# Linear attention into a one-of-eight expert layer on one core: where the scatters of sorted rows stand in the unit loop, row products in pairs, denominators from two tensors

## The chip, the core and the metric

One core of one Trainium2 chip runs the whole program in one launch. The metric is the device time of an execution in microseconds; lower is better. The time before is the median of three runs. Engines are named as in the profile: PE is TensorE, DVE is VectorE, ACT is ScalarE, POOL is GpSimd, SP is SyncE.

## What is computed

Attention without a softmax over 8 batches, 8 heads, 576 positions and 64 features, then a layer in which each of the 4608 tokens goes to one of eight experts:

```python
def phi(x, c, s):                       # c, s: cosine and sine of the position
    r = np.maximum(x, 0.0)
    return np.concatenate([r * c, r * s], axis=-1)
kv = np.einsum('bhsf,bhsd->bhfd', phi(k), v)
num = np.einsum('bhsf,bhfd->bhsd', phi(q), kv)
den = np.einsum('bhsf,bhf->bhs', phi(q), phi(k).sum(2))[..., None] + 1e-06
x = (num / den), one row of 512 per token
e = argmax(x @ w_gate);  gate = softmax(x @ w_gate)[e];  eom = sigmoid(x @ w_output_gate)[e]
out = gate * eom * (relu(x @ w1[e]) @ w2[e])      # w1[e]: 512x1024, w2[e]: 1024x512
```

## The kernel before

**Stages.** The program has two stages that overlap at their seam. In the attention stage the 4608 tokens are 36 units of 128 rows, four groups of nine units, two batches to a group; `n` is the unit's place in its group, 0 to 8. In the expert stage 39 tiles of 128 sorted rows pass through `layer1` and `layer2`. The tiles 0 to 10 (`EARLY`) are made up of rows of the first two groups alone; tile 11 is the first that may hold rows of the last group, so its fetch waits until all the scatters of that group have landed.

**A unit** (the loop over `units` at the end of the function) issues, in this order: `q_mm` (PE products of q with kv at L515, their evacuation by ACT at L520 and DVE at L522 into one of two buffers `u`), `aheads(i + 1)` (the weighting of the next unit's k: `k_ahead`, a `tensor_scalar` on DVE at L343 for each of two or three chunks, or an activation on ACT at L340), the transposes of q two units ahead, then the scatters that stand in this unit, `q_out` where `n` is 1, 3, 5, 7 or 8, and at the end the PE products of k and v (`k_do`, L378) and the loads. In the last group there is no k left to weight.

**q_out** turns a pair of units into rows. DVE adds 1e-6 to the denominators (L542, a `tensor_scalar` on 128x16), takes the reciprocal (L543), and makes the gate logits (L554, L558). POOL multiplies each unit's 512 columns by the reciprocals into `xrows` (L530, `q_rows`), which I call a row product: two of them for `n` = 1, 3, 5, 7 and one for `n` = 8. `between` puts one scatter between the two.

**Routing.** When the nine units of a group are done, `route` computes each row's expert and place in small DVE steps over the next units (L570 to L616). Nine scatters of one group's rows (`scatter`, L629, an indirect DMA on POOL of 128 rows of 516 two-byte words) then run during the next group, from xrows to the sorted table `xs` in DRAM. xrows has two buffers, so the first write of a later group (L541) waits until the scatters from that buffer have landed.

**Loads.** q, k, v and the rows of a tile (`fetch`, L763) are loaded by SP's queue. The weights of an expert (`load_w`, 16 loads of 1 MB at L237 and L240) are issued by POOL, in the same instruction stream and on the same software DMA queue as the scatters and as the writes of the output rows (L874). `wload` names the unit behind which each load stands: the first behind unit 22, the second behind 23, then 25, 27, 29, 31 and 33. I write W1, W2, ... for them in this order.

**What sets the order.** Each engine runs its instructions in the order in which the Python code issues them (`manual_schedule`). Two tables say how many scatters stand in a unit: `nsc` for the second and third group, `nsc2` for the last. Before, with the scatter between the two row products added, the nine scatters of a group stand at `n` = 3, 4, 5, 6, 7, 8 with 2, 1, 2, 1, 2, 1 of them.

Of the kernel before, what the change touches and what calls it, by code (L numbers as in the profile page):

```python
# [16 lines left out]
ALU = mybir.AluOpType  # L17
# [5 lines left out]
def kernel(  # L23
# [14 lines left out]
    DVE = nc.vector  # L38
# [234 lines left out]
    if True:  # L273
# [63 lines left out]
        def k_ahead(b, c, act):  # L337

            if act:
                ACT.activation(kcs[:, :, c, :], kbuf[b % 2][:, :, c, :], AF.Relu,  # L340
                               scale=cosc[:, c:c + 1])
                return
            DVE.tensor_scalar(kcs[:, :, c, :], kbuf[b % 2][:, :, c, :], cosc[:, c:c + 1],  # L343
                              0.0, ALU.mult, ALU.max)

# [189 lines left out]

        def q_out(g, u, glog, xrows, slot, n, between=None, late=None):

            rc = wk.tile([P, 2 * H], F32, name=f"rc{g}_{slot}", tag="rc")
            m = n * H
            if slot == 0:  # L540
                GP.tensor_copy(xrows[:, :, DM:DM + 2].bitcast(I32), ids[:, g, :].unsqueeze(2))  # L541
            DVE.tensor_scalar_add(rc[:, 0:m], u[:, 0:m, 64], 1e-6)  # L542
            DVE.reciprocal(rc[:, 0:m], rc[:, 0:m])  # L543
            for x in range(n):
                if x and between:
                    between()
                if late is None:
                    q_rows(GP, u, rc, xrows, slot, x)
                else:
                    late.append((u, rc, xrows, slot, x))  # L550
# [69 lines left out]

        def scatter(g, c):

            di, meta, xrows, c0, c1 = scat[g]
            if c == c0:
                GP.tensor_copy(xrows[:, c0:c1, DM + 2:DM + 4].bitcast(F32),
                               meta[:].unsqueeze(2))
            else:
                GP.nop()
            d = GP.indirect_dma_start(  # L629
                out=xs[:, :],  # L630
                out_offset=bass.IndirectOffsetOnAxis(ap=di[:, c - c0:c - c0 + 1], axis=0),
                in_=xrows[:, c, :], in_offset=None)


            tc.declare_no_dep(d.ins, group="sc", reason="distinct rows")
            tc.declare_no_dep(d.ins, group="early", reason="distinct rows")
            tc.add_to_no_dep_group("sc", d.ins)
            if g == NG - 1:
                last_sc.append(d.ins)
# [272 lines left out]

        def aheads(i):
            for n, x in enumerate(kwork[i] if i < NU else ()):
                k_ahead(*x, 20 <= i <= 27 and n == 1)

# [55 lines left out]

        nsc = {3: 1, 4: 1, 5: 1, 6: 1, 7: 1, 8: 1}
        nsc2 = {3: 1, 4: 2, 5: 1, 6: 1, 7: 1}
        outs = []
        for i, (b, c) in enumerate(units):
# [13 lines left out]
            q_mm(i, u, c % 2)  # L990
            aheads(i + 1)
            if i + 2 < NU:
# [18 lines left out]

            def scatter_next():
                nonlocal scd
                if scd < GC:
                    scatter(g - 1, scd)
                    scd += 1

            if g > 0:
                for _ in range((nsc2 if g == 3 else nsc).get(n, 0)):
                    scatter_next()  # L1020
            if c == 4 or c % 2 == 1:
                slot = 8 if c == 4 else 4 * (b % 2) + c - 1
                out_args = (g, u, glog, xrows, slot, 1 if c == 4 else 2,
                            scatter_next if g > 0 and n in (3, 5, 7) else None)
                if i < NU - 2:
                    q_out(*out_args)
                else:
                    outs.append(out_args)
            assert n < 8 or i == NU - 1 or g == 0 or scd == GC
            if n == 8:  # L1030
# [144 lines left out]
```

## Time and profile before

| what | value |
|---|---|
| three runs | 315.11 us median, 313.14 to 316.8 |
| the profiled execution | 313.45 us |
| its span, first to last instruction | 311.6 us |
| granted TensorE clock, mean | 0.984 |
| PE busy | 280.5 us (90%) |
| ACT busy | 179.9 us (58%) |
| DVE busy | 175.7 us (56%) |
| POOL busy | 130.2 us (42%) |

The profiled execution is 1.66 us under the median of the runs, and 1.85 us of it lie outside the span. The attention stage takes about the first 149 us and the expert stage the rest. A busy engine is not always a working one: an instruction that is held on its way counts as busy for as long as it is held, so the length of one instruction against the usual length of its group is as telling as the idle time.

### The profile page before, as it was taken

The page shows a single profiled execution, that of the slowest core. Times are in us where ns is not written, and L with a number is a line of the kernel's source. Part 1 is how long each engine was busy: PE and PEld are TensorE (multiplying, and loading weights), DVE is VectorE, ACT ScalarE, POOL GpSimd, SP SyncE. Part 2 cuts the span into 40 slices and gives each one's busy share as a digit, 9 for nine tenths or more (in the row PEclk, how much of TensorE's full clock was granted, in tenths as well). Part 3 has the DMA queues.
Part 4 walks back from the last instruction along what each step waited for, and adds up shares of the span by engine and source line. Part 5 has one row for each costly group of instructions (what it writes and reads, how often), then busy time and mean ns, then how long its engine had stood idle before and what let it go on. Part 6 is the DMA issues. An engine that isn't in the chain of part 4 may idle for free. (4 is left out here: it accounts for less than half of the span.)

```text
span 311.6 us, 10152 instructions
## 1 busy us (share of the span) xinstructions
PE 280.5 (90%) x3615; PEld 179.8 (58%) x3615; DVE 175.7 (56%) x510; ACT 179.9 (58%) x355; POOL 130.2 (42%) x169
## 2 busy tenths in 40 slices
PE   6788799899998877997989899999999999999991
PEld 2667687687777656765545445555544444444450
DVE  7536767789998999897688313333312222222231
ACT  4388689897989887875532333334354444444420
POOL 7003333147854878078766734062122222231322
PEclk9799799999999999999999999999999999999997
DMA  7999677869795899999998899999997878776522
GB/s 252 361 389 360 182 196 242 287 188 327 234 352 162 258 267 271 249 207 265 245 226 251 144 247 255 241 243 243 281 272 175 180 187 167 185 180 148 152 68 82
DMA packets 50976, 71.84 MB, mean 231 GB/s; under 512 B 23374, under 2 KB 30062, under 8 KB 49904
## 3 DMA queue, kind: packets, MB, share of 16 engines
q1 hardware_dynamic: 40608, 40.17, 44.7%
q0 software_dynamic: 10320, 31.01, 41.0%
q8 instruction: 32, 0.52, 0.7%
q14 instruction: 16, 0.13, 0.1%
HBM read 67.58 MB, written 16.17 MB: 269 GB/s over the span
## 5 line engine op out<-in xcount | busy, mean ns | idle before, releaser
L863 PE MATMUL yp<-wt,hts 128*128 x312 | 73.4, 379 | 0.1
L829 PE MATMUL hp<-wt,xts 128*128 x304 | 71.8, 379 | 1.2 <-issue 1.2
L839 ACT ACTIVATE hs<-hp 128x1024 f16<-128x1024 f32 x38 | 38.9, 1024 | 43.9 <-PE hp L829 43.9
L530 POOL TENSOR_TENSOR xr<-wt,rc 128x512 f16<-128x512 f32 x33 | 37.1, 1133 | 48.4 <-DVE rc L543 48.1
L870 DVE TENSOR_SCALAR ysp<-yp,xg 128x512 f32<-128x512 f32 x24 | 18.0, 751 | 69.7 <-PE yp L863 69.7
L515 PE MATMUL qo<-kvm,wt 64*64 64x162 f32 x1024 | 44.6, 306 | 8.6 <-DVE wt L522 3.4
L863 PEld LDWEIGHTS <-hts 128*128 128x128 f16 x312 | 30.4, 98 | 36.4 <-DMA hts<-hs 0.5
L794 ACT COPY xts<-xtsp 128x512 f16<-128x512 f16 x39 | 22.8, 586 | 44.5 <-PE xtsp L778 41.9
L378 PE MATMUL kvp<-wt 64*64 64x132 f32 x1152 | 42.4, 286 | 5.8 <-DVE wt L350 3.3
L829 PEld LDWEIGHTS <-xts 128*128 128x128 f16 x312 | 29.1, 98 | 29.8 <-issue 1.2
L520 ACT ACTIVATE wt<-qo,cosq 128x324 f32<-128x324 f32 x72 | 36.1, 530 | 14.8 <-PE qo L515 14.4
L522 DVE SCALAR_TENSOR_TENSOR wt<-qo,sinq,wt 128x324 f32<-128x324 f32 x72 | 36.9, 550 | 12.9 <-ACT wt L520 11.0
L515 PEld LDWEIGHTS qo<-kvm,wt 64*64 64x64 f32 x1024 | 35.5, 134 | 13.0 <-DVE wt L522 5.8
L378 PEld LDWEIGHTS kvp<-wt 64*64 64x64 f32 x1152 | 34.2, 137 | 11.6 <-issue 4.7
L874 POOL DMA_INDIRECT out_dram<-ysp,sidx x17 | 16.8, 986 | 46.5 <-DVE sidx L798 36.8
L333 ACT ACTIVATE wt<-wt,tanc 128x256 f32<-128x256 f32 x63 | 28.4, 513 | 1.3 <-DMA wt<-in_v_dram 1.3
L870 DVE TENSOR_SCALAR ysb<-yp,xg 128x512 f32<-128x512 f32 x15 | 11.2, 750 | 27.8 <-PE yp L863 27.8
L343 DVE TENSOR_SCALAR wt<-wt,cosc 128x256 f32<-128x256 f32 x56 | 24.4, 477 | 0.0
L480 ACT ACTIVATE qr<-wt 128x512 f32<-128x512 f32 x32 | 20.7, 646 | 3.6 <-DMA wt<-in_q_dram 3.6
L874 POOL DMA_INDIRECT out_dram<-ysb,sidx x11 | 10.8, 984 | 26.1 <-DVE ysb L870 14.6
L492 PE MATMUL qtp<-ident,qr 128*128 128x128 f32 x128 | 21.3, 290 | 0.2 <-ACT wt L333 0.2
L495 ACT COPY wt<-qtp 128x512 f32<-128x512 f32 x32 | 18.9, 590 | 1.7 <-PE qtp L492 1.2
(262 smaller groups left out, 312.2 us busy)
## 6 DMA issues: line engine op xcount, KB each, us to landing
wt<-in_moe_w_dram POOLq DMA_DIRECT2D x16, 1024.0 KB, 12.9
wt<-in_k_dram SPq DMA_DIRECT2D x16, 576.0 KB, 9.1
wt<-in_v_dram SPq DMA_DIRECT2D x16, 576.0 KB, 7.5
wt<-in_q_dram SPq DMA_DIRECT2D x16, 576.0 KB, 11.1
xg<-xs SPq DMA_DIRECT2D x43, 129.0 KB, 6.7
xs<-zt SPq DMA_DIRECT2D x9, 129.0 KB, 6.2
hts<-hs SPq DMA_TRANSPOSE x19, 3.3
out_dram<-ysp,sidx POOLq DMA_INDIRECT x17, 3.0
```

Of the source, the lines that this page charges most:

```text
L333: d = ACT.activation(tvs[:, c, :, 1:65], vbuf[b % 2][:, :, c, :], AF.Copy, scale=tanc[:, c:c + 1])
L343: DVE.tensor_scalar(kcs[:, :, c, :], kbuf[b % 2][:, :, c, :], cosc[:, c:c + 1], 0.0, ALU.mult, ALU.max)
L378: mm = PE.matmul(outs(i, mp), kcs[rows, m, c, :], mov, start=first, stop=(c == NCH - 1), skip_group_check=True)
L515: PE.matmul(qo[64 * l:64 * l + 64, 2 * mp + ih, 0:162], qT[r, hf, ih, l, :], kvms[b if c < 4 else b - 1 + l][r, n0:n0 + 2, :], start=True, ...
L520: d0 = ACT.activation(t, qo[:, :, 0:81], AF.Copy, scale=cosq[:, c:c + 1])
L522: d1 = DVE.scalar_tensor_tensor(u[:, h0:h0 + 4, :], qo[:, :, 81:162], sinq[:, c:c + 1], t, ALU.mult, ALU.add)
L530: e.tensor_tensor(xrows[:, slot + x, 0:DM].bitcast(F16).rearrange("p (h d) -> p h d", d=D), u[:, 8 * x:8 * x + 8, 0:64], rc[:, 8 * x:8 * x ...
L829: mm = PE.matmul(hps[fh], xts[:, kc, :], wt[:, bass.ds(ev, 1), kc * F + fh * 512:kc * F + fh * 512 + 512], start=(kc == 0), stop=(kc == 3))
L839: ACT.activation(hv, hp.rearrange("p (q c) -> p c q", c=8), AF.Relu)
L863: mm = PE.matmul(yp, hts[:, fc, :], wt[:, bass.ds(ev, 1), 4 * F + fc * DM:4 * F + fc * DM + DM], start=(fc == 0), stop=(fc == 7))
L870: DVE.tensor_scalar(ysb, yp, xg[:, DM + 2:DM + 4].bitcast(F32), None, ALU.mult)
L874: d = GP.indirect_dma_start(out=out[:, :], out_offset=bass.IndirectOffsetOnAxis(ap=idx, axis=0), in_=ysb, in_offset=None, bounds_check=N - ...
```

## The change

It does three things. `scatter` gets a further argument, the last weighting of k that DVE does in this unit, and waits for it by a semaphore. The scatters are issued at the end of a unit's `q_out`, three at a time, at `n` = 4, 6 and 8 (in the last group 4, 6 and 7, where no weighting is left to wait for), and no longer between the two row products. And the denominators come from a `scalar_tensor_tensor`, (u + 1e-6) times a tensor of ones, in place of `tensor_scalar_add`.

```diff
@@ k_ahead
             if act:
                 ACT.activation(kcs[:, :, c, :], kbuf[b % 2][:, :, c, :], AF.Relu,
                                scale=cosc[:, c:c + 1])
-                return
-            DVE.tensor_scalar(kcs[:, :, c, :], kbuf[b % 2][:, :, c, :], cosc[:, c:c + 1],
-                              0.0, ALU.mult, ALU.max)
+                return None
+            return DVE.tensor_scalar(kcs[:, :, c, :], kbuf[b % 2][:, :, c, :],
+                                     cosc[:, c:c + 1], 0.0, ALU.mult, ALU.max).ins
@@ q_out
-            DVE.tensor_scalar_add(rc[:, 0:m], u[:, 0:m, 64], 1e-6)
+            DVE.scalar_tensor_tensor(rc[:, 0:m], u[:, 0:m, 64], 1e-6, onesf[:, 0:m],
+                                     ALU.add, ALU.mult)
             DVE.reciprocal(rc[:, 0:m], rc[:, 0:m])
             for x in range(n):
-                if x and between:
-                    between()
@@ scatter
-        def scatter(g, c):
+        def scatter(g, c, behind=None):
...
+            if behind is not None:
+                tc.add_manual_dep(d.ins, behind.name, mybir.DependencyInfo(
+                    mybir.DependencyClass.Sync, mybir.DependencyReason.DATA),
+                    reason="behind the weighting of k")
@@ the loop over units
-        nsc = {3: 1, 4: 1, 5: 1, 6: 1, 7: 1, 8: 1}
-        nsc2 = {3: 1, 4: 2, 5: 1, 6: 1, 7: 1}
+        nsc = {4: 3, 6: 3, 8: 3}
+        nsc2 = {4: 3, 6: 3, 7: 3}
...
-            aheads(i + 1)
+            weighted = aheads(i + 1)
...
-            if g > 0:
-                for _ in range((nsc2 if g == 3 else nsc).get(n, 0)):
-                    scatter_next()
...
+            if g > 0:
+                for _ in range((nsc2 if g == 3 else nsc).get(n, 0)):
+                    scatter(g - 1, scd, weighted)
+                    scd += 1
```

Two places show what this does to POOL's instructions. The first is the third group, from its pair of row products at `n` = 3 to W2. Before, POOL has there:

```order
L530 TENSOR_TENSOR xr_1627<-wt,rc_2_1910 128x512
L629 DMA xs<-xr_1000,di@1_0_1851 36992x516
L231 TENSOR_LOAD ordi
...
L237 DMA wt<-in_moe_w_dram 128x4x1024
L629 DMA xs<-xr_1000,di@1_0_1851 36992x516
L530 TENSOR_TENSOR xr_1627<-wt,rc_4_2060 128x512
L629 DMA xs<-xr_1000,di@1_0_1851 36992x516
L530 TENSOR_TENSOR xr_1627<-wt,rc_4_2060 128x512
...
L240 DMA wt<-in_moe_w_dram 128x4096
```

After the change POOL has, from the same pair on (line numbers of `scatter` are one less):

```order
L530 TENSOR_TENSOR xr_1627<-wt,rc_2_1908 128x512 x2
L624 COPY xr_1000<-meta@1_0_1854 128x9
L628 DMA xs<-xr_1000,di@1_0_1851 36992x516 x3
L231 TENSOR_LOAD ordi
...
L237 DMA wt<-in_moe_w_dram 128x4x1024
L530 TENSOR_TENSOR xr_1627<-wt,rc_4_2058 128x512 x2
...
L240 DMA wt<-in_moe_w_dram 128x4096
L628 DMA xs<-xr_1000,di@1_0_1851 36992x516 x3
```

The three scatters ahead of W1 (L237) stand together right in front of it, behind the weighting of k of that unit, where before two of them were issued earlier and apart. W1 itself keeps its place behind the third scatter, and the pair of row products follows it as a whole.

The second place is the seam, on POOL again, from the fourth group's pair at `n` = 5 over W7 (L237) to the second write of output rows (L874). Before:

```order
L530 TENSOR_TENSOR xr_2305<-wt,rc_4_2785 128x512
L629 DMA xs<-xr_1627,di@2_0_2625 36992x516
...
L237 DMA wt<-in_moe_w_dram 128x4x1024
L629 DMA xs<-xr_1627,di@2_0_2625 36992x516 x2
L625 COPY xr_2305<-meta@3_0_3005 128x4
L629 DMA xs<-xr_2305,di@3_0_3002 36992x516 x2
...
L240 DMA wt<-in_moe_w_dram 128x4096
L874 DMA out_dram<-ysb_3100,xg_2315 4608x512
L629 DMA xs<-xr_2305,di@3_0_3002 36992x516 x2
L874 DMA out_dram<-ysb_3202,xg_2326 4608x512
```

And after the change:

```order
L530 TENSOR_TENSOR xr_2305<-wt,rc_4_2781 128x512 x2
L628 DMA xs<-xr_1627,di@2_0_2625 36992x516 x3
...
L237 DMA wt<-in_moe_w_dram 128x4x1024
L628 DMA xs<-xr_1627,di@2_0_2625 36992x516 x3
L624 COPY xr_2305<-meta@3_0_3005 128x4
L628 DMA xs<-xr_2305,di@3_0_3002 36992x516 x2
...
L240 DMA wt<-in_moe_w_dram 128x4096
L877 DMA out_dram<-ysb_3100,xg_2315 4608x512
L628 DMA xs<-xr_2305,di@3_0_3002 36992x516 x2
L877 DMA out_dram<-ysb_3202,xg_2326 4608x512
```

One scatter of the third group's rows has moved from ahead of W7 to behind it, and all six scatters now follow the pair at `n` = 5, where before three of them stood ahead of its second product.

## Rows read from the trace of the kernel before

**Rows 1.** A stretch: length, busy PE PEld DVE ACT POOL, clock, DMA share, GB/s

```profile
192.00:306.00 114.00, 113.15 (x665) 56.89 (x662) 32.86 (x70) 46.11 (x57) 31.04 (x33) 1.00 0.82 196
```

**Rows 2.** Timeline of PE: start, length, instruction, count, idle time before and its releaser

```profile
108.42 1.33 PE L515 MATMUL qo<-kvm,wt 64*64 64x162 f32 x32 [0.98 <-DVE wt L522]
...
113.70 0.77 PE L442 MATMUL kvtp<-ident,wt 128*128 128x128 f32 x4 [0.69 <-DVE wt L425]
...
116.08 1.33 PE L515 MATMUL qo<-kvm,qTt 64*64 64x162 f32 x32 [0.55 <-DVE wt L522]
...
121.32 0.93 PE L515 MATMUL qo<-kvm,wt 64*64 64x162 f32 x20 [1.68 <-DVE kvm L463]
```

**Rows 3.** The same of PE in the last group

```profile
142.07 1.19 PE L515 MATMUL qo<-kvm,wt 64*64 64x162 f32 x28 [1.65 <-DVE wt L522]
```

**Rows 4.** The weighting of k by itself: duration in ns, least, median, greatest

```profile
L343 DVE TENSOR_SCALAR wt<-wt,cosc x56: 340/347/1898, 21.4 to 124.3; 128x256 f32<-128x256 f32 x56
```

**Rows 5.** Timeline of DVE, third group and start of the fourth

```profile
104.78 0.77 DVE L343 TENSOR_SCALAR wt<-wt,cosc 128x256 f32<-128x256 f32 x1
...
111.42 1.90 DVE L343 TENSOR_SCALAR wt<-wt,cosc 128x256 f32<-128x256 f32 x1
...
119.09 1.89 DVE L343 TENSOR_SCALAR wt<-wt,cosc 128x256 f32<-128x256 f32 x1
...
121.10 0.46 DVE L542 TENSOR_SCALAR rc<-wt 128x8 f32<-128x8 f32 x1
...
136.67 1.01 DVE L522 SCALAR_TENSOR_TENSOR wt<-qo,sinq,wt 128x324 f32<-128x324 f32 x2
...
137.81 1.44 DVE L573 TENSOR_TENSOR sh@3_0_2735<-glog,lmax@3_0_2733 128x32 f32<-128x32 f32 x1
...
139.84 1.70 DVE L582 TENSOR_TENSOR oh<-iota8m,ei@3_0_2740 128x32 f16<-128x32 f32 x1
```

**Rows 6.** Timeline of POOL: scatters, row products and weight loads

```profile
105.55 1.01 POOL L629 DMA_INDIRECT xs<-xr,di@1_0_1851  x1 [0.17 <-issue]
106.56 0.82 POOL L237 DMA_DIRECT2D wt<-in_moe_w_dram  x1
...
119.76 1.06 POOL L530 TENSOR_TENSOR xr<-wt,rc 128x512 f16<-128x512 f32 x1
120.75 0.81 POOL L237 DMA_DIRECT2D wt<-in_moe_w_dram  x1
...
133.60 0.20 POOL L541 COPY xr<-ids 128x9 int32<-128x9 int32 x1 [9.10 <-DMA xs<-xr,di@1_0_1851]
...
139.37 1.04 POOL L629 DMA_INDIRECT xs<-xr,di@2_0_2625  x1 [0.18 <-issue]
140.42 1.07 POOL L530 TENSOR_TENSOR xr<-wt,rc 128x512 f16<-128x512 f32 x1
...
152.72 0.96 POOL L629 DMA_INDIRECT xs<-xr,di@2_0_2625  x1 [0.30 <-issue]
...
165.07 0.99 POOL L874 DMA_INDIRECT out_dram<-ysb,xg  x1 [1.24 <-DMA xs<-xr,di@2_0_2625]
```

**Rows 7.** DMA queues from 100 to 110 us: packets, MB, share of 16 engines

```profile
q1 hardware_dynamic: 945, 2.05, 71.6%
q0 software_dynamic: 100, 0.28, 7.9%
```

**Rows 8.** The same from 110 to 134 us

```profile
q0 software_dynamic: 1601, 4.62, 89.6%
```

**Rows 9.** Waits of SP's queue: what waited for what, us in total, times, longest

```profile
SPq L763 <- DMA xs<-xr,di@3_4_3187: 12.0, 1, 12.0
```

**Rows 10.** Timeline of SP at the fetch of tiles 11 and 12

```profile
184.18 1.50 SPq L763 DMA_DIRECT2D xg<-xs  x2
```

**Rows 11.** The fetch by itself, all tiles: time to landing

```profile
DMA to landing us min/median/max: 2.1/6.7/11.2
```

**Rows 12.** Timeline of PE: the transposes of tile 11

```profile
191.87 0.39 PE L778 MATMUL xtsp<-ident,xg 128*128 128x128 f16 x4
```

More of the change, by code (lines that the diff above doesn't have):

```diff
@@ L534, in q_rows, with q_out @@
                 ALU.mult)
-        def q_out(g, u, glog, xrows, slot, n, between=None, late=None):
+        def q_out(g, u, glog, xrows, slot, n, late=None):
             rc = wk.tile([P, 2 * H], F32, name=f"rc{g}_{slot}", tag="rc")
@@ L913, in aheads @@
         def aheads(i):
+            last = None
             for n, x in enumerate(kwork[i] if i < NU else ()):
-                k_ahead(*x, 20 <= i <= 27 and n == 1)
+                last = k_ahead(*x, 20 <= i <= 27 and n == 1) or last
+            return last
         def k_do(i):
@@ L1010 @@
                 next(first_half)
[L1012 to L1016, printed above, removed]
-            if g > 0:
-                for _ in range((nsc2 if g == 3 else nsc).get(n, 0)):
-                    scatter_next()
             if c == 4 or c % 2 == 1:
                 slot = 8 if c == 4 else 4 * (b % 2) + c - 1
-                out_args = (g, u, glog, xrows, slot, 1 if c == 4 else 2,
-                            scatter_next if g > 0 and n in (3, 5, 7) else None)
+                out_args = (g, u, glog, xrows, slot, 1 if c == 4 else 2)
                 if i < NU - 2:
```

## Prediction

> **What bounds the kernel now.** I read the stretches first. From 192 us on PE is busy 113.15 of 114.00 us [rows 1]: the expert stage from tile 11 to the end is PE's and nothing in the change touches it. So the end moves by as much as tile 11 moves, which starts at 191.87 [rows 12]. Two chains meet there, and the later one decides.
>
> Chain A is PE's own work before it. PE's timeline shows where PE stood waiting for DVE in the third and fourth group: 0.98 + 0.69 + 0.55 + 1.68 + 1.65 = 5.55 us [rows 2, 3]. DVE's timeline shows why: a weighting of k takes 0.35 us [rows 4], but 0.77, 1.90 and 1.89 in front of these waits, and two steps of the routing with two inputs in SBUF take 1.44 and 1.70 [rows 5]. POOL's timeline beside it: the weighting of 119.09 ends at 120.98, just behind the row product that began at 119.76 and took 1.06, and the step of 139.84 lasts through the rest of a scatter, 139.37 to 140.41, and through the row product on its heels until 141.49 [rows 5, 6]. DVE is held while POOL runs a scatter and the row product behind it, both in one.
>
> Chain B is the software DMA queue. Tile 11 may hold rows of the last group, so SP's queue stood 12.0 us for the last scatter before it fetched it at 184.18 [rows 9, 10]. With the median 6.7 us to landing [rows 11] the rows are there at 190.9, 1.0 us before PE wants them. So B has 1.0 us of room, and whatever A gains is worth 1.0 us at most unless B moves as well. B reaches back far: the queue shows 89.6% of the engines' time from 110 to 134 us, 4.62 MB or 0.19 MB per us [rows 8], and 7.9% from 100 to 110 [rows 7]. It fills up with W1, issued at 106.56, and from there POOL waits for landings: 9.10 us for the second group's last scatter until 133.60, and 1.24 us at 165.07 [rows 6].
>
> **The change, part by part.** The work is the same: 27 scatters in the unit loop, 20 denominators, the same row products and loads. What it moves:
>
> Chain A. Without a scatter between, a pair of row products takes 2 x 1.06 = 2.1 us from the reciprocal on, against 1.06 + 0.17 + 1.01 + 1.06 = 3.3.
> - PE's wait at 108.42: the weighting at 104.78 was held 0.77 - 0.35 = 0.42 us by a row product that now ends earlier. Some of it goes back to the scatters that now stand there; I take 0.3 us back.
> - 113.70 and 116.08: the weighting at 111.42 was held 1.55. Now W1 is out only at 109.6 (below), the pair follows until 111.7, and the weighting, due at about 111.1, is still held some 0.7. Returned: 0.6.
> - 121.32: held 1.54 at 119.09. The pair at n = 7 now stands behind three scatters and ends some 0.8 into the weighting. Returned: 0.75.
> - 142.07: the two steps were held 1.2 and 1.5. The pair still runs through the first of them; what is behind it should be free. Returned between 0.6 and 1.65, I take 1.1.
>
> The sum is 2.75 us; the bounds are 0 (every hold replaced by another) and 5.55. From it goes a new wait. The fourth group's first row products stand behind the copy of 133.60, which waits for the landing; by chain B this comes 1.4 later, at 135.0, the first product ends at 135.0 + 0.2 + 1.06 = 136.3, and L522 of unit 31 has to write the same buffer. Before, that L522 stood at 136.67 [rows 5]; moved up by 0.3 + 0.6 + 0.75 = 1.65 it would stand at 135.0. So 1.3 go back, and A reaches tile 11 at 191.87 - 1.45 = 190.4.
>
> The denominators cost nothing: 128x16 by one instruction as before. As a tensor_scalar the one at 121.10 took 0.46 and ended with the weight load that POOL issued from 120.75 to 121.56 [rows 5, 6], so some 0.3 a time is at stake. The Trainium skill says (SBUF — State Buffer, "Who interferes with whom") that a DVE instruction with two SBUF inputs meets only those GpSimd instructions that read SBUF; by that rule the new form would run freely beside scatters. The trace agrees only in part: the two-input step at 139.84 lasted on beside the scatter of 139.37 and ended with the row product [rows 5, 6], so a scatter with a row product on its heels does hold it. By the rule another 0.3 us would come back on chain A, by the row nothing; neither reaches the sum, which chain B sets.
>
> Chain B. Three scatters in a row take 3 x 1.00 + 2 x 0.30 = 3.6 us. They now wait for the weighting of unit 22, which is over at 104.78 + 0.35 = 105.1, so the third is out at 108.8 and W1 at 108.8 instead of 106.56: 2.2 later, and queued behind it are all further loads and row products. The queue does not feel all of it, as it was nearly empty until 110 while SP's loads held 71.6% of the engines [rows 7]. What it does feel is that two of the three scatters, 128 x 1032 bytes = 0.132 MB each, now fall into the stretch that is full: 2 x 0.132 / 0.19 = 1.4 us. Bounds: 0 (the queue would not have started earlier anyhow) and 2.2. I take 1.4. In the fourth group one scatter moves from ahead of W7 to behind it: 0.132 / 0.19 = 0.7 earlier. But then the instruction that POOL waits with at 165.07, the eighth software DMA behind the first scatter after W7 (counted in the two orders of the second place), is a scatter now and not the output write behind it: 0.97 + 0.30 = 1.3 more, bounds 0 and 1.3. Sum 1.4 - 0.7 + 1.3 = +2.0, and I take it that POOL has no slack from 165 us to the last scatter. Rows of tile 11 at 190.9 + 2.0 = 192.9.
>
> A is there at 190.4, B at 192.9: tile 11 starts 1.0 us late. 313.45 + 1.0 = 314.45 for the profiled execution; the median of the runs lies 1.66 above, so I say 316.1. A measurement of this kernel can tell about 1% from no change, 3.1 us, so this is no change.
>
> **The rivals.** *The gain is kept.* The fetch of a tile has landed in as little as 2.1 us [rows 11]. If tile 11's rows come 4.6 us faster than the median, B is at 188.3 and does not bind; and if the pairs hold the weighting no more, about 60% of the 5.55 us returns, 3.3. 311.8 in the frame of the runs. For it: the holds are plain to see and pairs end early. Against: the software queue is full around that fetch as well, and the unit 31 wait must not come either.
>
> *POOL carries its lateness through: slower.* After the change nine scatters (1.3 us each with their gap), two weight loads and a pair follow the pair at n = 3, and the third group's last scatter goes out at about 156 to 157 and not at 152.72 [rows 6]: 3.3 late. I let this vanish into the landings that POOL waits for before 165.07. If those landings are as late as POOL is, it stays, and with the 1.3 and the 1.0 us of room the end is 3.3 + 1.3 - 1.0 = 3.6 later: 318.7. It decides from the point where POOL's output write waits no longer for a landing at 165.07. Against: it is the full queue that POOL waits for at 133.60 and at 165.07, so the queue is the later of the two.
>
> *The scatters hold as before and the queue takes no notice.* The weighting meets a scatter's issue in the next unit, as three of them last 3.6 us and a unit without its waits some 3.3, (121.32 - 108.42 - 0.69 - 0.55 - 1.68) / 3; the row of 121.10 says that an issue alone holds a tensor_scalar. Then A gains nothing, and with W1's delay swallowed B is at 190.9 - 0.7 + 1.3 = 191.5, still inside its room: no change, 315.1.
>
> **How the numbers follow.** Forecast 0.50, the third rival 0.20, the gain kept 0.14, POOL late 0.16. The forecast and the third rival lie within 1%; a fifth of the first rival too. Faster 0.12, within 1% 0.72, slower 0.16. The range leaves out little of either outer rival: 311.6 to 318.8.
>
> **What would show it.** Right: no weighting of k in the second and third group over 1.2 us; W1 at 108 to 109.5; the copy L541 of the fourth group at 134 to 136; PE idle in front of tile 11 waiting for its rows; the end within 2 us of before. Wrong: W1 not later, or L541 not later; PE not waiting for tile 11's rows, so that the gain of chain A stands in the end; or a fetch of tile 11 behind 188.

## The result, and the profile after

The changed kernel takes 320.96 us (median of 5 runs, 319.72 to 321.2), the kernel before on the same chip 316.8 us (5 runs, 313.14 to 319.55): 1.0139 times the time before, 95% interval 1.0096 to 1.0182. It is slower, where I had forecast no change. All ratios below are to the kernel before in the same call on the same chip, since chips differ: its medians were 316.8, 323.6, 322.7, 314.2, 322.6 and 321.6 us in the six calls. A ratio leaves out executions over 1.5% above the fastest of their kernel: with all executions `e4_wfirst`, `c_after` and `e12_g3only` would stand at 1.020, 1.018 and 1.009, and the profiled executions of these three and of `e1_den`, `e2_nowait` and `e13_w1late` are among those left out.

The profiled executions have spans of 319.4 and 311.6 us, 7.8 apart. Some 3.3 us of that belong to the execution of before, which lay that far below its median of 316.8; the changed one's, 321.2, lay at its own.

POOL's timeline of the changed kernel, second to last group (columns as in [rows 6]):

```profile
92.36 0.96 POOL L628 DMA_INDIRECT xs<-xr,di@0_0_1224  x1 [0.30 <-issue]
98.26 0.20 POOL L541 COPY xr<-ids 128x9 int32<-128x9 int32 x1 [4.94 <-DMA xs<-xr,di@0_0_1224]
...
109.42 1.03 POOL L628 DMA_INDIRECT xs<-xr,di@1_0_1851  x1 [2.29 <-DVE ti@e L724]
...
113.01 0.81 POOL L237 DMA_DIRECT2D wt<-in_moe_w_dram  x1
...
122.42 0.83 POOL L237 DMA_DIRECT2D wt<-in_moe_w_dram  x1
...
127.15 0.99 POOL L628 DMA_INDIRECT xs<-xr,di@1_0_1851  x1 [0.30 <-issue]
...
140.02 0.20 POOL L541 COPY xr<-ids 128x9 int32<-128x9 int32 x1 [11.29 <-DMA xs<-xr,di@1_0_1851]
...
143.02 2.07 POOL L530 TENSOR_TENSOR xr<-wt,rc 128x512 f16<-128x512 f32 x2
...
159.25 0.96 POOL L628 DMA_INDIRECT xs<-xr,di@2_0_2625  x1 [0.30 <-issue]
```

This answers to [rows 6]. W1 is 6.45 us later (113.01 against 106.56), the last group's copy L541 6.42 (140.02 against 133.60), the last of the nine scatters that run during that group 6.53 (159.25 against 152.72). From W1 on the lateness is handed down POOL's own instructions at nearly full size. And it begins earlier than I looked: the last scatter of the second group's last block goes out at 92.36, and the third group's copy L541 waits 4.94 us for it to land.

DVE's timeline of the changed kernel, weightings and a denominator of the third group, and two steps of the fourth, as in [rows 5]:

```profile
108.30 0.34 DVE L343 TENSOR_SCALAR wt<-wt,cosc 128x256 f32<-128x256 f32 x1
...
114.31 0.75 DVE L343 TENSOR_SCALAR wt<-wt,cosc 128x256 f32<-128x256 f32 x1
...
120.99 1.65 DVE L343 TENSOR_SCALAR wt<-wt,cosc 128x256 f32<-128x256 f32 x1
122.76 0.15 DVE L542 SCALAR_TENSOR_TENSOR rc<-wt,onesf 128x8 f32<-128x8 f32 x1
...
141.25 1.02 DVE L522 SCALAR_TENSOR_TENSOR wt<-qo,sinq,wt 128x324 f32<-128x324 f32 x2 [0.80 <-POOL xr L530]
...
142.40 2.75 DVE L572 TENSOR_TENSOR sh@3_0_2733<-glog,lmax@3_0_2731 128x32 f32<-128x32 f32 x1
```

In the third group the holds did go, in part: 0.34, 0.75 and 1.65 stand where 0.77, 1.90 and 1.89 stood, and the denominator takes 0.15 where it took 0.46. In the fourth they did not: one routing step takes 2.75, through to the end of the pair that POOL runs from 143.02 to 145.09, where two took 1.44 and 1.70. PE's timeline shows what took their place, as in [rows 2, 3]:

```profile
88.19 1.33 PE L515 MATMUL qo<-kvm,wt 64*64 64x162 f32 x32 [0.98 <-DVE rc L542]
...
104.32 1.33 PE L515 MATMUL qo<-kvm,wt 64*64 64x162 f32 x32 [1.26 <-DVE rc L542]
...
122.98 1.33 PE L515 MATMUL qo<-kvm,wt 64*64 64x162 f32 x32 [1.44 <-DVE rc L542]
...
133.92 0.65 PE L492 MATMUL qtp<-ident,qr 128*128 128x128 f32 x4 [1.52 <-ACT qr L480]
...
139.11 1.33 PE L515 MATMUL qo<-kvm,wt 64*64 64x162 f32 x32 [0.48 <-DVE rc L542]
...
146.47 1.33 PE L515 MATMUL qo<-kvm,wt 64*64 64x162 f32 x32 [1.82 <-DVE wt L522]
...
151.30 1.33 PE L515 MATMUL qo<-kvm,qTt 64*64 64x162 f32 x32 [0.21 <-DVE wt L522]
...
197.09 0.40 PE L781 MATMUL xtsp<-ident,xg 128*128 128x128 f16 x4 [1.39 <-DMA xg<-xs]
198.15 3.35 PE L832 MATMUL hp<-wt,xts 128*128 x8 [0.66 <-issue]
```

The rows of 88.19, 104.32, 122.98, 139.11 and 151.30 are the first products of the units 18, 22, 27, 31 and 35. In the trace of before units 18, 27, 31 and 35 start at 86.25, 121.32 [rows 2], 134.65 and 146.89, as three more of its rows show:

```profile
86.25 1.33 PE L515 MATMUL qo<-kvm,wt 64*64 64x162 f32 x32 [0.56 <-ACT wt L333]
...
134.65 1.60 PE L515 MATMUL qo<-kvm,wt 64*64 64x162 f32 x32 [0.71 <-DVE kvm L463]
...
146.89 1.33 PE L515 MATMUL qo<-kvm,qTt 64*64 64x162 f32 x32 [0.21 <-DVE wt L522]
```

So PE is 1.94 us behind at unit 18, 1.66 at unit 27, 4.46 at unit 31 and 4.41 at unit 35. The 2.80 us from unit 27 to unit 31 are lost ahead of the copy L541, which runs at 140.02, so this copy can't be their reason. ACT's timeline shows it, before and after:

```profile
94.63 0.92 ACT L333 ACTIVATE wt<-wt,tanc 128x256 f32<-128x256 f32 x2 [0.60 <-DMA wt<-in_v_dram]
...
128.56 0.63 ACT L480 ACTIVATE qr<-wt 128x512 f32<-128x512 f32 x1 [1.08 <-DMA wt<-in_q_dram]
```

```profile
97.46 0.92 ACT L333 ACTIVATE wt<-wt,tanc 128x256 f32<-128x256 f32 x2 [1.50 <-DMA wt<-in_v_dram]
...
133.24 0.63 ACT L480 ACTIVATE qr<-wt 128x512 f32<-128x512 f32 x1 [4.11 <-DMA wt<-in_q_dram]
```

ACT waits 4.11 us for the last load of q, before 1.08, and PE waits 1.52 for ACT at 133.92. SP issues this load at the same place in both, 29.8 and 29.9 us behind unit 18, but W1 and W2 now leave POOL 5.0 and 2.1 us ahead of it, before 9.6 and 3.1. That these two hold the load up is argued from this order; `e13_w1late`, where W1 and W2 stand 3.0 and 2.2 us ahead of it and nothing else is moved, has ACT waiting 2.24 us for it, against 0.20 in `c_before`.

Then comes tile 11. SP's timeline, as in [rows 10], and two stretches of the core, columns as in [rows 1]:

```profile
190.60 5.38 SPq L766 DMA_DIRECT2D xg<-xs  x5
```

```profile
197.00:201.50 4.50, 3.75 (x13) 1.57 (x14) 0.22 (x1) 0.58 (x1) 2.81 (x4) 0.66 1.14 271
201.50:306.00 104.50, 104.05 (x614) 52.45 (x613) 28.40 (x63) 44.44 (x55) 27.04 (x28) 1.00 0.86 201
```

The fetch goes out at 190.60 (before 184.18 [rows 10]) and PE stands 1.39 us for the rows, where before it had not waited [rows 12]. Behind that wait the granted clock has a mean of 0.66 over 4.5 us, in part the lower of its two levels (1.2 and 2.4 GHz), and the eight products of `hp` take 3.35 us instead of 1.89. From the transposes of tile 11 to those of tile 12 it is 6.65 us (197.09 to 203.74), before 4.25 (191.87 to 196.12): 2.40 more. The sum of the profile is 1.94 up to unit 18, 2.47 from there to unit 35, -0.58 to tile 11 without its wait, 1.39 for the wait, 2.40 behind it and 0.13 to the end: 7.75 us.

### The profile page after: what moved, and what is told of

Same layout as the page of the kernel before. It is cut to its first block, busy times and chain, and to the rows that moved or that the text cites. A ratio compares the mean times of both kernels' runs of the same rounds, so it can differ in the third digit from the quotient of the medians.

```text
span 319.4 us, 10154 instructions
## 1 busy us (share of the span) xinstructions
PE 280.7 (88%) x3615; PEld 178.1 (56%) x3615; DVE 169.8 (53%) x510; ACT 179.9 (56%) x355; POOL 129.6 (41%) x169
## 5 line engine op out<-in xcount | busy, mean ns | idle before, releaser
L832 PE MATMUL hp<-wt,xts 128*128 x304 | 73.3, 385 | 1.1 <-issue 1.1
L515 PE MATMUL qo<-kvm,wt 64*64 64x162 f32 x1024 | 44.2, 307 | 11.5 <-DVE rc L542 4.5
L797 ACT COPY xts<-xtsp 128x512 f16<-128x512 f16 x39 | 22.7, 585 | 46.6 <-PE xtsp L781 43.2
L522 DVE SCALAR_TENSOR_TENSOR wt<-qo,sinq,wt 128x324 f32<-128x324 f32 x72 | 37.0, 551 | 21.7 <-ACT wt L520 15.6
L378 PE MATMUL kvp<-wt 64*64 64x132 f32 x1152 | 40.6, 277 | 6.8 <-issue 3.3
L515 PEld LDWEIGHTS qo<-kvm,wt 64*64 64x64 f32 x1024 | 35.1, 135 | 16.3 <-DVE wt L522 6.1
L378 PEld LDWEIGHTS kvp<-wt 64*64 64x64 f32 x1152 | 32.4, 132 | 12.9 <-issue 6.8
L343 DVE TENSOR_SCALAR wt<-wt,cosc 128x256 f32<-128x256 f32 x56 | 20.0, 399 | 0.0
```

The lines of the kernel that those rows point to most:

```text
L378: mm = PE.matmul(outs(i, mp), kcs[rows, m, c, :], mov, start=first, stop=(c == NCH - 1), skip_group_check=True)
L515: PE.matmul(qo[64 * l:64 * l + 64, 2 * mp + ih, 0:162], qT[r, hf, ih, l, :], kvms[b if c < 4 else b - 1 + l][r, n0:n0 + 2, :], start=True, ...
L522: d1 = DVE.scalar_tensor_tensor(u[:, h0:h0 + 4, :], qo[:, :, 81:162], sinq[:, c:c + 1], t, ALU.mult, ALU.add)
L797: ACT.copy(xts[:].rearrange("p k t -> p (k t)"), xp16)
L832: mm = PE.matmul(hps[fh], xts[:, kc, :], wt[:, bass.ds(ev, 1), kc * F + fh * 512:kc * F + fh * 512 + 512], start=(kc == 0), stop=(kc == 3))
```

## The experiments

### Parts of the change

`e1_den`: the kernel before with the new denominators alone. `e2_nowait`: the changed kernel without the wait for the weighting.

```diff
-            DVE.tensor_scalar_add(rc[:, 0:m], u[:, 0:m, 64], 1e-6)
+            DVE.scalar_tensor_tensor(rc[:, 0:m], u[:, 0:m, 64], 1e-6, onesf[:, 0:m],
+                                     ALU.add, ALU.mult)
```

```diff
-                    scatter(g - 1, scd, weighted)
+                    scatter(g - 1, scd)
```

> The kernel before with the denominators from two tensors alone. Theory (the lateness comes from the place of the scatters and W1 behind them): no change, within 0.5% of before, W1 at 106 to 109 and the copy L541 of the fourth group at 132 to 136. Rival (the new form is itself held beside scatters, or frees DVE): 1 us or more either way, with L542 rows of over 0.5 us or PE's waits for DVE in the third group 1 us shorter.

> The changed kernel without the wait of the scatters for the weighting of k; their places stay. Theory: the wait held the first three scatters of the third group for 2.3 us in front of W1, so W1 is out at about 110.7 and not at 113.0, and the whole software queue, the copy L541 of the fourth group and the fetch of tile 11 come 2.3 us earlier: ratio to before about 1.006. Rival (the place alone costs, the wait is hidden): like the changed kernel, 1.013. Second rival (the wait protects the weighting): over 1.015, with rows of L343 over 1.2 us again.

Measured: 1.0036 (0.9984 to 1.0089) and 1.0133 (1.0063 to 1.0204). The denominators do nothing that can be told from no change, and the loss does not hang on the wait. What is left is the placement: blocks of three, and pairs. How much of a ratio is chance shows in `c_before` below: the same code as the kernel before, at 0.9942.

### The place of the blocks in the changed kernel

`e3_early`: blocks at `n` = 3, 5, 7, right behind the pair. `e4_wfirst`: the weight loads ahead of a unit's scatters. `e5_ahead`: blocks at 3, 5, 7 ahead of `q_out`. `e6_spread`: two and one scatters in turn, as before, but all behind the pair. `c_before` and `c_after` are the two kernels again.

```diff
-        nsc = {4: 3, 6: 3, 8: 3}
-        nsc2 = {4: 3, 6: 3, 7: 3}
+        nsc = {3: 3, 5: 3, 7: 3}
+        nsc2 = {3: 3, 5: 3, 7: 3}
```

```diff
-        nsc = {4: 3, 6: 3, 8: 3}
-        nsc2 = {4: 3, 6: 3, 7: 3}
+        nsc = {3: 2, 4: 1, 5: 2, 6: 1, 7: 2, 8: 1}
+        nsc2 = {3: 2, 4: 2, 5: 2, 6: 1, 7: 2}
```

In `e4_wfirst` the five lines that issue a unit's scatters stand behind its loads; in `e5_ahead` the first four of them stand ahead of the `if` that sets `out_args`, with the first table.

> The changed kernel with each block of three scatters one unit earlier (n = 3, 5 and 7 in all groups), behind the pair of row products of that unit and with its wait. Theory (late blocks make the next group's copy L541 wait and put three scatters in front of W1): the copy of the third group at 94 to 95 and not at 98.3, W1 at 105 to 108, the copy of the fourth group at 132 to 135, ratio to before 0.995 to 1.003. Rival (pairs and blocks as such are slow, by the holds of DVE beside them): the ratio stays at 1.01 or more, with PE's waits for DVE as in the changed kernel.

> The changed kernel with each unit's scatters behind its weight load and not in front of it; nothing else. Theory (W1's time sets the software queue, and the queue sets the copy L541 of the fourth group and tile 11): W1 at 107 to 109 and not at 113.0, the copy of the fourth group at 134 to 136, the fetch of tile 11 at 184 to 187, ratio to before 1.000 to 1.005. Rival (what counts is when the last scatter of a group is out, not W1): the copy stays at 139 or later and the ratio at 1.012 or more.

> The kernel before, for its trace beside the others on the same chip. Ratio 0.995 to 1.005; W1 about 5 us behind the start of unit 22, and row products that wait 48 to 53 us in all for the reciprocals.

> The changed kernel, for its trace on the same chip. Ratio 1.010 to 1.018; W1 8 to 9 us behind the start of unit 22, and row products that wait 55 to 60 us in all for the reciprocals.

> The changed kernel with its blocks of three at n = 3, 5 and 7 and ahead of the unit's row products (between the transposes and q_out), where the run with early blocks had them behind the row products; the wait for the weighting stays. Theory (POOL stands idle in front of each pair until the reciprocals are there, and scatters ahead of the pair use that time, scatters behind it come late): row products wait under 52 us, W1 within 5.5 us of the start of unit 22, ratio 0.996 to 1.005. Rival (blocks of three or pairs cost by themselves): the ratio stays at 1.010 or more.

> The changed kernel with as many scatters in each unit as before (2, 1, 2, 1, 2, 1 from n = 3 on, in the last group 2, 2, 2, 1, 2), all behind the pair and with the wait. Theory (what counts is behind or ahead of the pair): row products wait 55 us or more, ratio 1.006 to 1.016. Rival (the blocks of three cost): 0.997 to 1.004.

Measured: `e3_early` 1.0206 (1.0114 to 1.0298), `e4_wfirst` 1.0115 (0.9997 to 1.0234), `c_before` 0.9942 (0.9872 to 1.0012), `c_after` 1.0108 (1.0009 to 1.0207), `e5_ahead` 1.0357 (1.0283 to 1.0432), `e6_spread` 1.0075 (1.0008 to 1.0143). Earlier blocks do not help, though they bring W1 forward: from unit 18 to W1 it is 20.8 us in `e5_ahead` against 24.8 in the changed kernel, and it is the slowest of all. Its L541 of the last group is the earliest of all the kernels, 43.5 us behind unit 18, and yet its unit 35 the latest, at 66.3: its unit 27 starts 40.3 us behind unit 18 already, where the changed kernel has 34.8. So there is a second cost beside POOL's lateness; I take it to be the row products that stand behind the blocks, but no run has that alone. In `e6_spread` the second group's last scatter goes out 2.6 us behind unit 18 instead of 4.2 in the changed kernel, and the ratio is the lowest of these variants, still above 1. But it does not break the blocks up: no instruction of POOL stands between the two scatters of one unit and the one of the next, so in the second group three still go out in a row twice (72.79, 74.17, 75.47 and 80.74, 82.18, 83.44), and only the last three have a row product between them.

### Single moves from the kernel before

`e7_pair`: the scatter between the two row products goes behind them. `e8_behind`: the scatters ahead of `q_out` go behind it. `e9_w1`: the weight loads go ahead of a unit's scatters and row products. `e13_w1late`: W1 one unit later, nothing else moved.

```diff
-                if x and between:
-                    between()
...
+            if between:
+                between()
```

```diff
+            for w in wload.get(i, ()):
+                load_w(*w)
             if g > 0:
                 for _ in range((nsc2 if g == 3 else nsc).get(n, 0)):
...
-            for w in wload.get(i, ()):
-                load_w(*w)
```

```diff
-        wload = {22: [(0, 0)], 23: [(0, 1)], 25: [(1, 0)], 27: [(1, 1)], 29: [(2, 0)],
+        wload = {23: [(0, 0), (0, 1)], 25: [(1, 0)], 27: [(1, 1)], 29: [(2, 0)],
```

> The kernel before with the scatter that stood between two row products put right behind the second; all others stay. Theory (the change loses because the first scatter of a unit no longer runs while POOL waits for the reciprocals, and the software queue starts late; a pair as such costs nothing): W1 19 to 20.5 us behind the start of unit 18, 4 MB through the software queue 36.5 to 38.5 us behind it, ratio to before 0.996 to 1.004. Rival (pairs in a row cost by themselves): 1.006 or more.

> The kernel before with the scatters that stood ahead of q_out behind it; the one between two row products stays. Theory (the place ahead of the pair is what counts): W1 20.5 to 23 us behind the start of unit 18, 4 MB through the software queue at 38 to 41, ratio 1.003 to 1.010. Rival (blocks of three cost, and here are none): 0.997 to 1.002.

> The kernel before with each unit's weight load ahead of its scatters. Theory (the software queue lies idle until W1 and is full from there): W1 18 to 19.3 us behind the start of unit 18, the queue about 1 us earlier at 4 MB, ratio 0.994 to 1.000. Rival (the copy L541 waits for the last scatter, which now has more weights ahead of it in the queue): L541 of the fourth group 48 us or more behind unit 18, ratio over 1.002.

> The kernel before with the first weight load, W1, one unit later (behind unit 23, directly ahead of W2); no scatter and no row product moves. Theory (the software queue starts late and nothing makes it up): W1 at 26 to 27.5 us behind unit 18, 4 MB at 39.5 to 42, the copy L541 of the fourth group at 50 to 52.5, ratio 1.007 to 1.015. Rival (blocks of three and late pairs cost by themselves, through DVE and the buffers of u and xrows): 0.998 to 1.003.

Measured: 0.9999 (0.9967 to 1.0031), 1.0003 (0.9972 to 1.0033), 1.0022 (0.9992 to 1.0053), and for `e13_w1late` 1.0027 (0.9987 to 1.0067). Pairs and the side of the row products, each moved alone, cost and bring nothing that can be told; these three runs were on the chip with the median of 314.2. In `e13_w1late` W1 is a unit late, and with it all that the queue carries behind it; that costs at most 0.7% on its chip, one of the slower. My theory at that time, that the whole loss is W1's lateness as the software queue takes it, fell with it for these chips; on the faster ones W1 was not moved alone.

### Group by group

Five kernels have the changed placement (blocks, pairs and wait) in some groups only: `e10_last` in the last (made from the kernel before, with its denominators; that group has no wait), and four made from the changed kernel by a switch `old` on the group's number `g`, which is 1 in the second group, and by the tables of before (`nsc0`, `nsc1`) where it is set: `e12_g3only` in the third, `e14_g2only` in the second, `e11_g3before` in the second and last, `e15_g2before` in the third and last. `c2_after` is the changed kernel again.

```diff
+            old = g in (2, 3)
+            if old:
+                for _ in range((nsc1 if g == 3 else nsc0).get(n, 0)):
+                    scatter_next()
...
-                            scatter_next if g > 0 and n in (3, 5, 7) else None)
+                            scatter_next if old and n in (3, 5, 7) else None)
...
+            if g > 0 and not old:
+                for _ in range((nsc2 if g == 3 else nsc).get(n, 0)):
+                    scatter(g - 1, scd, weighted)
+                    scd += 1
```

These are the lines of `e14_g2only` against the kernel before; `old` is `g in (1, 3)` in `e12_g3only`, `g == 2` in `e11_g3before` and `g == 1` in `e15_g2before`.

> The kernel before with the changed placement in the last group alone (blocks of three at n = 4, 6 and 7 behind the row products, no scatter between; no wait; denominators as before). Theory (the loss comes from the second and third group, where the queue starts): the queue as before until 6.4 MB, ratio 1.000 to 1.005. Rival (the last group's blocks carry the loss to tile 11): 1.008 or more, with the last scatter of all over 91 us behind unit 18.

> The changed kernel with the third group's scatters and row products as before (one scatter ahead of the pair, one between, no wait); second and last group, and the denominators, as changed. Theory (the loss arises in the third group, where three scatters and W1 have to be out before the loads of q, k and v leave the DMA engines free): W1 19 to 21 us behind unit 18, 4 MB of the software queue at 36 to 38.5, ratio 0.995 to 1.003. Rival (the second or the last group's blocks lose too): 1.006 or more.

> The kernel before with the changed placement, pairs and wait in the third group alone (denominators as changed, which cost nothing by themselves). Theory: W1 23 to 25.5 us behind unit 18, 4 MB at 39.5 to 42, ratio 1.008 to 1.015, the whole loss of the change. Rival (it takes the late copy L541 of the third group, which comes from the second group's last block): under 1.005.

> The changed kernel on the same chip as the three others. Ratio 1.010 to 1.016; W1 24 to 25.5 us behind unit 18, 4 MB at 41 to 42.

> The kernel before with the new denominators, and the changed placement (row products in pairs, blocks of three scatters behind a unit's weighting, last one behind n=8, the wait) in the second group alone; third and last group as before. Theory (the loss arises in the second group): 1.006 to 1.015 times the kernel before, unit 22 16 us or more behind unit 18 where kernels without the blocks there have 14.5 to 15.2, the last scatter of the second group about 4 us behind unit 18's start, and the third group's copy of the sorted rows waiting for it. Rival (each group's blocks alone cost next to nothing, and only together do they cost): within 1.004.

> The changed kernel with the second group as before (singles, scatters ahead of a unit's output products, no block of three there); third and last group and the denominators as changed. Theory (the loss arises in the second group): 1.000 to 1.005 times the kernel before, unit 22 14.5 to 15.2 us behind unit 18. Rival (it takes blocks in several groups, whichever they are): 1.005 to 1.012, about half of the changed kernel's loss.

Measured, with times in us behind the first product of unit 18 in the profiled execution:

| kernel | changed in | last scatter of third group | L541 of last group | unit 35 | tile 11 | ratio |
|---|---|---|---|---|---|---|
| `c_before` | none | 34.9 | 46.1 | 60.0 | 111.6 | 0.9942 |
| `e14_g2only` | second | 36.5 | 47.9 | 61.8 | 112.9 | 1.0021 (0.9978 to 1.0064) |
| `e12_g3only` | third | - | - | - | - | 1.0038 (0.9989 to 1.0087) |
| `e15_g2before` | third, last | 38.1 | 49.6 | 62.0 | 115.8 | 1.0108 (1.0052 to 1.0165) |
| `e11_g3before` | second, last | 36.9 | 48.2 | 62.8 | 117.0 | 1.0209 (1.0154 to 1.0263) |
| `c2_after` | all | 41.5 | 53.1 | 65.5 | 120.5 | 1.0214 (1.0164 to 1.0264) |
| kernel before | none | 35.6 | 47.4 | 60.6 | 105.6 | 1 |
| `e10_last` | last | 35.4 | 46.9 | 61.6 | 105.9 | 0.9962 (0.9919 to 1.0006) |
| changed kernel | all | 39.0 | 51.8 | 63.1 | 108.9 | 1.0139 (1.0096 to 1.0182) |

The last three were profiled on the two faster chips, the others on slower ones, where tile 11 comes some 6 us later in the kernel before too, partly in waits between the expert tiles; they are to be read against `c_before`. In all the traces of this case PE waits for the rows of tile 11 in one only, the changed kernel's first.

The rows behind three lines of the table, from the timelines of PE and POOL. `c_before`, `e14_g2only`, `e15_g2before`, in this order; for the first and the last with W1 (L237) and the products of unit 28 (126.03, and 124.44 to 127.24) and unit 31 (136.42 and 136.39):

```profile
88.85 1.33 PE L515 MATMUL qo<-kvm,wt 64*64 64x162 f32 x32 [1.31 <-DVE rc L542]
...
108.47 0.81 POOL L237 DMA_DIRECT2D wt<-in_moe_w_dram  x1
...
123.77 1.00 POOL L629 DMA_INDIRECT xs<-xr,di@1_0_1851  x1 [0.31 <-issue]
...
126.03 1.28 PE L515 MATMUL qo<-kvm,wt 64*64 64x162 f32 x32
...
134.92 0.20 POOL L541 COPY xr<-ids 128x9 int32<-128x9 int32 x1 [8.52 <-DMA xs<-xr,di@1_0_1851]
...
136.42 1.63 PE L515 MATMUL qo<-kvm,wt 64*64 64x162 f32 x32 [0.49 <-DVE kvm L463]
...
148.85 1.33 PE L515 MATMUL qo<-kvm,qTt 64*64 64x162 f32 x32 [0.41 <-issue]
```

```profile
87.13 1.30 PE L515 MATMUL qo<-kvm,wt 64*64 64x162 f32 x32
...
123.64 0.99 POOL L630 DMA_INDIRECT xs<-xr,di@1_0_1851  x1 [0.30 <-DMA xs<-xr,di@1_0_1851]
...
134.99 0.20 POOL L541 COPY xr<-ids 128x9 int32<-128x9 int32 x1 [8.73 <-DMA xs<-xr,di@1_0_1851]
...
148.91 1.33 PE L515 MATMUL qo<-kvm,qTt 64*64 64x162 f32 x32 [0.43 <-issue]
```

```profile
87.43 1.33 PE L515 MATMUL qo<-kvm,wt 64*64 64x162 f32 x32 [1.22 <-DVE rc L542]
...
110.66 0.81 POOL L237 DMA_DIRECT2D wt<-in_moe_w_dram  x1
...
124.44 1.05 PE L515 MATMUL qo<-kvm,wt 64*64 64x162 f32 x13
...
125.58 0.97 POOL L630 DMA_INDIRECT xs<-xr,di@1_0_1851  x1 [0.30 <-issue]
...
125.74 0.51 PE L515 MATMUL qo<-kvm,wt 64*64 64x162 f32 x3 [0.25 <-issue]
126.50 0.47 PE L515 MATMUL qo<-kvm,wt 64*64 64x162 f32 x2 [0.25 <-DVE oh@2_0_2484 L578]
127.24 0.82 PE L515 MATMUL qo<-kvm,wt 64*64 64x162 f32 x14 [0.27 <-issue]
...
136.39 1.46 PE L515 MATMUL qo<-kvm,wt 64*64 64x162 f32 x32 [0.49 <-DVE rc L542]
...
137.03 0.20 POOL L541 COPY xr<-ids 128x9 int32<-128x9 int32 x1 [9.89 <-DMA xs<-xr,di@1_0_1851]
...
149.38 1.54 PE L515 MATMUL qo<-kvm,qTt 64*64 64x162 f32 x32
```

The reader is to see three things. First, the blocks of one group make POOL late and those of two groups later still: against `c_before` the third group's last scatter is 1.6 us later with the second group changed (123.64 - 87.13 = 36.51, against 34.92), 3.2 with the third changed, and 6.6 with all (on the faster chip, 3.3 with all).

Second, L541 keeps its distance from W1 where the order of loads and blocks stays. It comes 26.4 to 26.7 us behind W1 in these three kernels (W1 at 108.47, 108.33 and 110.66), and 27.0 behind it in the kernel before and in the changed one. From the third group's last scatter it is 11.1 to 12.9 us in these five and in `c2_after`, but this distance is not kept elsewhere: in `e5_ahead` the scatter is later than in `c_before` (36.7) and L541 earlier (43.5), 6.8 us behind it; in `e13_w1late` the scatter stands where it stood (34.9), W1 is 6.5 us later and L541 4.1. So the wait at L541 is a wait for the queue that W1 starts, and not only for the scatter. W1 is not all of it either: where the loads or the blocks are moved against each other (`e3_early`, `e4_wfirst`, `e5_ahead`, `e9_w1`, `e13_w1late`) L541 comes 22.7 to 29.9 us behind W1.

Third, on the slower chips the units are late by something else than L541. In `e15_g2before` unit 31 is 1.4 us later behind unit 18 than in `c_before`, and starts at 136.39, ahead of L541 at 137.03. What is late is unit 28: its 32 products come in four pieces, from about the issue of the third group's last scatter (125.58) on, and last from 124.44 to 128.06, 3.6 us instead of 1.3. So do those of the unit behind each block of a changed second or third group on these chips: 2.4, 3.3 and 3.5 us at the units 15, 17 and 19 in `e14_g2only`, 3.2, 2.6 and 3.6 at 24, 26 and 28 in `e15_g2before`, and all six in `c2_after`, while in `c_before` none behind unit 10 takes over 1.7. At the last block of a group this is what PE loses: from unit 19 to 20 it is 6.2 us in `e14_g2only` and 3.9 in the two others, from unit 28 to 29 6.2 us in `e15_g2before` and 4.1 in `c_before`. In the changed kernel's first profile, on a faster chip, no unit between 18 and 35 is broken up; what comes late there are the loads of v and q, as shown above for q.

The theory that the second group alone is at fault, which I had reached by elimination, is refuted by `e14_g2only`: its L541 and its unit 35 are both 1.8 us later than in `c_before`, and it costs nothing that can be told, with an interval up to 0.6%, 2.1 us. Both runs came out as the rival had it, that it takes the blocks of several groups; by the traces each group adds its own delay.

Several things stay open. `e11_g3before`, the second and last group, has a ratio of 1.0209 on record, but the lowest three of its six executions (324.42, 326.37 and 328.19 us) lie only 1.1% above the mean of before (322.7), so its loss may be half of that. And from unit 35 to tile 11 it is 51.6 us in `c_before` and 51.1 in `e14_g2only`, but 53.9 in `e15_g2before`, on the same chip as `e14_g2only`, 54.3 in `e11_g3before` and 55.0 in `c2_after`: 2 to 3 us more in the three kernels with a changed last group. Most of it is there by tile 4, which comes 14.6 and 14.4 us behind unit 35 in the first two and 16.5 to 17.0 in these three; the fetch of tile 11 has no part in it, as PE doesn't wait for its rows there. On the slower chips all nine kernels with a changed last group have ratios of 1.0075 or more, and the five without one 1.0038 or less. So the last group may be where most of the loss arises there. The last group was not changed alone on one of the slower chips, and on a faster one `e10_last` loses nothing, so I can't say whether it costs by itself or only behind a late group.

## Why the prediction was wrong

**The bound** was read rightly. Behind tile 11 PE is busy for 104.05 of 104.50 us, the end moves as tile 11 does, and tile 11 did wait for its rows, as forecast, in this execution; in the traces from the slower chips it doesn't.

**Chain B was mis-sized, in the step on W1.** I had the third scatter out and W1 at 108.8; W1 went out at 113.01. I counted the block itself rightly, 3.59 us from 109.42 to 113.01. But I let it start at 105.1, the end of the weighting in the trace of before, and it started at 109.42, 4.3 later: the weighting began at 108.30 and not at 104.78, 3.5 later, and the scatter followed its end at 108.64 only 0.78 later, a way I had put at nothing. The 3.5 are 1.94 of unit 18, 0.90 from there to unit 22 (16.13 us, before 15.23) and 0.68 within the unit. The 0.90 come from a load of v, for which ACT waits 1.50 us at 97.46, before 0.60; DVE and PE then wait for ACT in turn, PE 1.26 at unit 22 (104.32). That load runs beside the second group's last block, which the prediction never followed; that the block holds it up is not shown. The 1.94 can't be put down to the change: at unit 10, ahead of the first scatter, PE stands 2.85 us for nothing that the profile shows ("issue") in this execution, 1.21 in that of before, but 2.85 too in `e10_last`, where the first three groups are as before; and at unit 15 it stands 1.51 so, 0.56 in that of before, and 1.59 in `c_before`.

**"The queue does not feel all of it" failed.** I let 1.4 of 2.2 us reach L541. Measured from unit 18, W1 is 4.51 later, L541 4.48, the last of the nine scatters that run during the last group 4.59, the fetch of tile 11 4.48: nothing is swallowed on the way, and nothing gained by the W7 step. That L541 waits for the full queue was right: it stands 27.0 us behind W1 before and after. The error was to think that a full queue is free of POOL: POOL starts it with W1, and what W1 is late the queue passes on whole, in place of the 1.4 that I worked out from the two scatters. My rival "POOL carries its lateness through", at 318.7, came nearer; it lacked W1's full lateness, the loads and the clock.

**The loads on SP's queue** were not in the sum at all: I took their share of the engines [rows 7] as a reason why the queue would not feel W1, and not what a later W1 does to them. The last load of q keeps ACT waiting 4.11 us instead of 1.08, and the 2.80 us that are lost from unit 27 to unit 31 are more than all that PE falls behind from unit 18 to unit 35 (2.47).

**Chain A's gain was mis-sized.** I took 0.3 + 0.6 + 0.75 us back in the third group. The holds shrank (0.42, 1.55 and 1.54 to about 0, 0.4 and 1.3), the wait of 0.69 is gone and that of 1.68 is 1.44, but the wait of 1.26 at unit 22 is new. From unit 18 to 27 it is 34.79 us against 35.07: 0.28 gained of 1.65. In the last group I took 1.1 back and got nothing: the routing step at 142.40 is held for 2.75 us by the pair, and PE's wait behind it is 1.82 (146.47) where it was 1.65. The new wait of L522 for the late row product did come, 0.80 on DVE (141.25) where I had put 1.3. Unit 27 to 35 takes 2.75 longer where I had 1.3 - 1.1 = 0.2, and unit 31 has all of it.

**What tile 11's wait costs** was not in the sum: 1.39 us of waiting and 2.40 behind it, most of it by the clock. I had priced a late tile at its lateness alone.

**The denominators** cost nothing, as forecast. The new form takes 0.136 to 0.178 us in all 20 instances, the old one up to 1.690; the one at 122.76 took 0.15 beside the weight load that POOL issued from 122.42 to 123.25, where the old form had taken 0.46 beside one [rows 5, 6]. The Trainium skill (SBUF — State Buffer, "Who interferes with whom") has it that a DVE instruction with two SBUF inputs meets only those of GpSimd that read SBUF; in this row the trace agrees. `e1_den` shows that it brings no time.

By the signs I had named: the weighting over 1.2 us is there once (1.65), W1 and L541 are beyond their marks, the fetch is behind 188. The last three said that chain B was too short.

## What to carry to other kernels

When a queue bounds a chain, ask who starts it: an instruction that starts it late makes all of it late by as much (here 4.51 us at W1 and 4.48 at L541 and at the fetch), and the copy, products and scatters behind. Ask as well which loads of other queues then run beside it, and who waits for these (here ACT, 4.11 us instead of 1.08). Follow such delays through every group in which the code is run, also those far ahead of the critical place. Before a difference is put down to a copy or a landing, look whether the late instruction starts ahead of it (here unit 31, 0.9 us ahead of L541). And price a wait of PE with what the clock does behind it.

## What was not expected of the hardware

Where three scatters stand in a row, PE's stream on the slower chips breaks up into short pieces. Timelines of POOL and PE in `c2_after`, second group's last block and unit 19:

```profile
94.31 0.96 POOL L628 DMA_INDIRECT xs<-xr,di@0_0_1224  x1 [0.30 <-issue]
```

```profile
92.95 1.31 PE L515 MATMUL qo<-kvm,wt 64*64 64x162 f32 x16
94.51 0.43 PE L515 MATMUL qo<-kvm,wt 64*64 64x162 f32 x3 [0.25 <-issue]
95.28 0.50 PE L515 MATMUL qo<-kvm,wt 64*64 64x162 f32 x4 [0.34 <-issue]
96.03 0.69 PE L515 MATMUL qo<-kvm,wt 64*64 64x162 f32 x9 [0.25 <-issue]
```

The 32 products that take 1.33 us elsewhere take 3.77 (92.95 to 96.72), in pieces of 16, 3, 4 and 9 with 0.25 to 0.34 us between, from about the issue of the third scatter on; nothing in the profile is waited for. `e11_g3before` shows the same at its block of the second group, where the third scatter goes out at 90.10 and the first gap ends at 90.31. In the list of waits PE stands 7.2 us for "issue" in 18 instances at L515 in `c2_after`, and 2.9 in one in the changed kernel's first profile, on a faster chip. What stops PE there was not settled. It makes up the some 2.2 us that PE loses from unit 19 to 20 in `e14_g2only` and from unit 28 to 29 in `e15_g2before`; of the 2 to 3 us between unit 35 and tile 11 it is not shown to be a part.
